# A 32-head attention kernel with a gated MLP: prologue by tile with TensorE transposes, vector work kept off the head boundaries, last out-projection split by head

## Chip, cores, metric

One core of one Trainium2 chip. Times are device microseconds (us) of that core. Most runs of one kernel lie within 0.3% of each other; in two kernels (a_spq and a_best) one run lies up to 0.6% off. Every run quoted here was in the fast state. "Span" is the profiled time from the first to the last instruction, about 2 us less than that run's time. "Pitch" is the time from the start of one matmul to the start of the next.

## The reference, cut to what matters

```python
xn = layernorm(A_x)                                   # 2048 x 512
q = xn @ wq                                           # 32 heads of 128
p = softmax(q @ k_cache^T * 128**-0.5)                # per head, 2048 x 2048
s = concat_heads(p @ v_cache) @ wo                    # 2048 x 512
h = relu(xn @ w1 + b1) ** 2;  g = silu(h @ w2 + b2)   # F = 1792
return A_x + s * g                                    # bf16
```

## The kernel before

The queries come in 4 blocks of 512 rows. In each block all 32 heads are done in turn, each in 8 steps of 256 keys, so there are 1024 steps. A step is a pair of score matmuls (into `psA`), an exponential of 1024 elements per partition on ScalarE (into `pT`), and eight PV matmuls of 129 columns (into `psO`; the extra column of ones gives the softmax denominator). PV runs two steps behind the scores. Between scores and PV, TensorE takes "fillers": matmuls of the projections, the MLP and the output projection, in groups of 4, 8 or 14 into two PSUM banks (`psF`), each group ended by an eviction on VectorE (it reads the finished bank, so that the bank can be filled again). A "combine" is VectorE's last arithmetic on a row tile of the output: times the gate `g`, plus `A_x`.

```python
# the prologue: the whole block of 512 rows in one go
ln_load(0); fill_wq(0); fill_k(0); fill_wq(1)         # all on SP's DMA queue
ln_stats(0)                                           # 4 x bn_stats/bn_aggr, one power on GpSimd
ln_scale(0, range(TPB))                               # 4 x scale, each followed by a DMA transpose
fill_v(0); fill_k(1); fill_v(1); fill_wq(2)
tok_w1 = ...                                          # w1 in one transfer, then w2
# [cut: projections of heads 0 and 1]

for pi in range(NPAIR):                               # the 1024 steps
    g, k = divmod(pi, NPR)
    gen_scores(pi)
    credit = min(credit + left[0] / (NPAIR - pi), 8.0)
    n = 0
    while n < 3:
        late = bool(jobs) and jobs[0][0] + 8 <= pi
        if not (credit >= 1.0 or late) or n == 2 or not fill_one(pi):
            break                                     # fill_one: one filler; evicts after a group's last
        ...
    if pi >= LAG:
        gen_pv(pi - LAG)      # after a head's last PV: VectorE copies psO to o_un, frees psO
    # [cut: loads of later heads]
    for fn in events.pop(pi, []):                     # statistics, scalings, gates, combines
        fn()
# after the loop: the last PVs, the transpose of the last head, then what is left,
# 4 jobs of 8 matmuls (one for each 128 rows), one after the other
while jobs or cur[0] is not None or events:
    for fn in events.pop(step, []):
        fn()
    fill_one(step, force=True)
    step += 1
```

Every instruction goes into its engine's queue in this program order. VectorE's trace shows it working in that order: at the head boundary at 100 us in the kernel before, the copy to `o_un` starts at 99.58 us, behind four statistics and a cast, though the PV matmuls that it waits for ended at 97.5.

The softmax here doesn't subtract the row's maximum and nothing guards it: scores larger than these inputs give would overflow.

Of the kernel before, what the change touches and what calls it, by code (L numbers as in the profile page):

```python
# [9 lines left out]
P = 128  # L10
# [177 lines left out]


def _bn_stats(e, out, in_):  # L190
    return e.bn_stats(out, in_)  # L191
# [19 lines left out]
def bass_recurrent_scan__mha_block_cached__dense_activation_squared_relu__prompt_kernel(  # L211
# [70 lines left out]
    ve_t = sb("ve_t", [P, TPB], F32)  # L282
    mhalf = sb("mhalf", [P, TPB], F32)
    rstd = sb("rstd", [P, TPB], F32)
# [13 lines left out]
    sl_wq = [S.slot(f"wq{i}") for i in range(NSW)]  # L298
    sl_xl = S.slot("xl")
    sl_xT = [S.slot(f"xT{i}") for i in range(TPB)]  # L300
    sl_w1 = S.slot("w1")
    sl_w2 = S.slot("w2")
# [6 lines left out]
    sl_fin = [S.slot("fin0"), S.slot("fin1")]  # L309

    t_mhalf = E(GP, partial(_memset, out=mhalf[:], val=-0.5))
    t_ones = None
    for i in range(NSL):
        t_ones = E(GP, partial(_memset, out=v_sb[:, i, :, Dh:Dh + 1], val=1.0))


    t_xl = [None] * NQB
    t_xn_w = [None] * NQB
    tok_xT = [[None] * TPB for _ in range(NQB)]
    t_xr = [None] * NQB  # L320

    def ln_load(j):
        t_xl[j] = S.emit_dma(
            SP, partial(_dma, out=x_ln[:], in_=A_x[0, j * QB:(j + 1) * QB, :].rearrange(
                "(t p) d -> p t d", p=P)), sl_xl, deps=[t_xn_w[j - 1] if j else None])

    def ln_stats(j):
        t = None
        for i in range(TPB):
            ts_ = E(DV, partial(_bn_stats, out=st_t[:, i, :], in_=x_ln[:, i, :]),  # L330
                    deps=[t_xl[j], t_xn_w[j - 1] if j else None])
            t = E(DV, partial(_bn_aggr, out=mv_t[:, i, :], in_=st_t[:, i, :]), deps=[ts_])
        t = E(DV, partial(_ts, out=ve_t[:], in0=mv_t[:, :, 1], scalar1=LN_EPS, scalar2=None,
                          op0=ALU.add), deps=[t, t_xr[j - 1] if j else None])
        t_xr[j] = E(GP, partial(_tt, out=rstd[:], in0=ve_t[:], in1=mhalf[:], op=ALU.pow),
                    deps=[t, t_mhalf, t_xn_w[j - 1] if j else None])

    def ln_scale(j, tiles):
        for i in tiles:
            t_xn_w[j] = t = E(DV, partial(_ts, out=xn_t[:, i, :], in0=x_ln[:, i, :],  # L340
                                          scalar1=mv_t[:, i, 0:1], scalar2=rstd[:, i:i + 1],
                                          op0=ALU.subtract, op1=ALU.mult),
                              deps=[t_xr[j], tok_xT[j - 1][i] if j else None])
            jt = j * TPB + i
            tok_xT[j][i] = S.emit_dma(
                SP, partial(_dmaT, out=xnT[:, :, jt * P:(jt + 1) * P], in_=xn_t[:, i, :]),
                sl_xT[i], deps=[t])

# [23 lines left out]

    def fill_v(g):
        if g >= NG:
            return
        h, i, prev = g % H, g % NSL, g - NSL
        t_vfill[g] = S.emit_dma(
            SP, partial(_dma, out=v_sb[:, i, :, 0:Dh],
                        in_=A_v_cache[0, h].rearrange("(t p) d -> p t d", p=P)), sl_v[i],
            deps=[t_PV_last[prev] if prev >= 0 else None])  # L380

    def fill_wq(g):
        if g >= NG:
            return
        h, i, prev = g % H, g % NSW, g - NSW
        t_wqfill[g] = S.emit_dma(
            SP, partial(_dma, out=wq_sb[:, i, :, :],
                        in_=A_wq[:, h * Dh:(h + 1) * Dh].rearrange("(c p) e -> p c e", p=P)),
            sl_wq[i], deps=[t_proj[prev] if prev >= 0 else None])
# [88 lines left out]
    dbg = os.environ.get("KDBG")  # L478

    def at(step, fn):  # L480
        events.setdefault(step, []).append(fn)
# [20 lines left out]
    def job_h(j, c):  # L502
        js = slice(j * QB, (j + 1) * QB)
        box = [None]

        def mm(n, bank):
            box[0] = E(PE, partial(_mm, out=bankF(bank), lhsT=w1_sb[:, n, c * P:(c + 1) * P],
                                   rhs=xnT[:, n, js], start=(n == 0), stop=(n == NDC - 1)),
                       deps=[tok_w1, t_bankF[bank]] + tok_xT[j], inc=(n == NDC - 1))

        def evac(bank, step):
            s = c % 2
            t1 = E(DV, partial(_ts, out=r_t[:, s, :], in0=bankF(bank), scalar1=b1f[:, c:c + 1],
                               scalar2=0.0, op0=ALU.add, op1=ALU.max),
                   deps=[box[0], t_b1, t_rt[s]])
            t_h2[j, c] = t_rt[s] = E(
                DV, partial(_tt, out=h2T[:, c, :], in0=r_t[:, s, :], in1=r_t[:, s, :],
                            op=ALU.mult),
                deps=[t1] + [t_o2.get((j - 1, qt)) for qt in range(TPB)])
            return t1  # L520
        return NDC, mm, evac
# [34 lines left out]
    def job_wo(j, m, qt):  # L556
# [4 lines left out]
        def mm(n, bank):  # L561
            g = g0 + n
            box[0] = E(PE, partial(_mm, out=bankF(bank),
                                   lhsT=oT[:, g % NOT, qt * P:(qt + 1) * P],
                                   rhs=wo_all[:, m * HC + n, :], start=(n == 0),
                                   stop=(n == HC - 1)),
                       deps=[tok_wo[m], tok_oT[g], t_bankF[bank]], inc=(n == HC - 1))

        def evac(bank, step):
# [5 lines left out]
            elif m < NCH - 1:  # L575
                t_acc[qt] = t = E(DV, partial(_tt, out=acc[:, qt, :], in0=bankF(bank),
                                              in1=acc[:, qt, :], op=ALU.add),
                                  deps=[box[0], t_acc[qt]])
            else:
                s = jt % 2  # L580
                t = E(DV, partial(_stt, out=tmp_t[:, s, :], in0=bankF(bank), scalar=0.5,
                                  in1=g_all[:, jt % (2 * TPB), :], op0=ALU.mult, op1=ALU.mult),
# [18 lines left out]
    def pre_combine(j, qt):  # L601

        jt = j * TPB + qt
        t = E(DV, partial(_stt, out=acc[:, qt, :], in0=acc[:, qt, :], scalar=0.5,
                          in1=g_all[:, jt % (2 * TPB), :], op0=ALU.mult, op1=ALU.mult),
              deps=[t_acc[qt], t_g[jt]])
        t_u[jt] = E(DV, partial(_tt, out=acc[:, qt, :], in0=acc[:, qt, :], in1=x_t[:, qt, :],
                                op=ALU.add), deps=[t, tok_xt[jt]])
# [4 lines left out]
    for j in range(NQB):  # L613
        b = j * (SPB - NPR)
        for c in range(NFC):
# [6 lines left out]
        for m in range(NCH):  # L622
            for qt in range(TPB):
                r = b + HC * NPR * (m + 1) + 14
                jobs.append((r + 2 + 12 * qt, r, job_wo(j, m, qt)))
    jobs.sort(key=lambda x: x[0])
    cur = [None]
    bank_no = [0]

    def fill_one(step, force=False):  # L630
# [15 lines left out]
        else:  # L646
            cur[0][1] = i + 1
        return True


    ln_load(0)
    fill_wq(0)
    fill_k(0)
    fill_wq(1)
    ln_stats(0)
    ln_scale(0, range(TPB))
    fill_v(0)
    fill_k(1)
    fill_v(1)
    fill_wq(2)  # L660
    tok_w1 = S.emit_dma(SP, partial(_dma, out=w1_sb[:],
                                    in_=B_w1.rearrange("(c p) f -> p c f", p=P)), sl_w1)
    tok_b1 = S.emit_dma(GP, partial(_dma_gather, nc, out=b1b[:],
# [4 lines left out]
    for g in range(2):  # L668
        n, mm, evac = job_proj(g)
        for i in range(n):  # L670
            mm(i, g)
        t_bankF[g] = evac(g, 0)
    t_b1 = E(DV, partial(_copy, out=b1f[:], in_=b1b[:]), deps=[tok_b1])
    tok_w2 = S.emit_dma(SP, partial(_dma, out=w2_sb[:],
                                    in_=B_w2.rearrange("(c p) d -> p c d", p=P)), sl_w2)
    for i in range(NCH):
        at(3 * NPR + 6 + 2 * NPR * i, partial(load_wo, i))
    for j in range(NQB):
        if j + 1 < NQB:
            at(j * SPB + 3 * NPR, partial(ln_load, j + 1))  # L680
            at(j * SPB + 7 * NPR, partial(ln_stats, j + 1))
            for i in range(TPB):
                at(j * SPB + 10 * NPR + 6 + NPR * i, partial(ln_scale, j + 1, [i]))
        at(j * SPB + SPB // 2, partial(load_xt, j))
        for qt in range(TPB):
            at(j * SPB + SPB + 4 + 2 * qt, partial(pre_combine, j, qt))

    left = [sum(job[0] for _, _, job in jobs) - HC * TPB]
    credit = 0.0
    for pi in range(NPAIR):  # L690
# [3 lines left out]
        n = 0  # L694
        while n < 3:
            late = bool(jobs) and jobs[0][0] + 8 <= pi
            if not (credit >= 1.0 or late) or n == 2 or not fill_one(pi):
                break
# [3 lines left out]
        if dbg:  # L702
            print(pi, n, round(credit, 1), jobs[0][0] if jobs else None)
        if pi >= LAG:
# [6 lines left out]
        if k == LAG + 1 and g >= 1:  # L711
            gen_oT(g - 1)
        for fn in events.pop(pi, []):
            fn()
    for pi in range(NPAIR - LAG, NPAIR):
        gen_pv(pi)
    gen_oT(NG - 1)
    step = NPAIR
    while jobs or cur[0] is not None or events:
        for fn in events.pop(step, []):  # L720
            fn()
        fill_one(step, force=True)
        step += 1
    assert not jobs and cur[0] is None and not events

# [32 lines left out]
```

## Time and profile before

| | before |
|---|---|
| time, median of 3 runs | 1290.23 us (1288.71 to 1290.77) |
| span of the profiled run (a run of 1287.63 us) | 1285.8 us |
| first score matmul starts | 20.34 us |
| from there to the start of the last PV matmul | 1247.85 us |
| from there to the end of the last output sum | 12.95 us |
| from there to the end | 4.71 us |

The last four rows add up to the span. They are read from the timeline and are used for every run below: first scores = the prologue, stretch = the 1024 steps, end = the last output projection, rest = the last store.

### The profile page before, as it was taken

The numbers are of one execution on the slowest core, as the hardware profiler recorded it, in microseconds if no ns is written. First come the engines' busy times: TensorE is split into PE (matmuls) and PEld (weight loads), VectorE is DVE, ScalarE is ACT, GpSimd is POOL, SyncE is SP. The second block draws the span as 40 slices with busy tenths as digits, with TensorE's granted clock in tenths as the row PEclk, the third lists the DMA queues.
The fourth block names the chain that finished last, engine by engine and source line by source line (L and its number), as shares of the span: only waits on it lengthen the run. The fifth ranks groups of instructions, "written<-read, shape, count | busy, mean of one in ns | idle before, by whom it ended". The sixth has DMA issues, their size and how long they took to land.

```text
span 1285.8 us, 26303 instructions
## 1 busy us (share of the span) xinstructions
PE 1231.2 (96%) x11506; PEld 807.6 (63%) x11712; DVE 472.0 (37%) x949; ACT 1052.9 (82%) x1041; POOL 21.6 (2%) x42
## 2 busy tenths in 40 slices
PE   3999999999999999999999999999999999999997
PEld 1665666666666666666666666666666666666664
DVE  2443323323534433322353533332345343233234
ACT  1887888888887888888888888888888878888894
POOL 1000000000001000000000100000000000000000
PEclk8999999999999999999999999999999999999999
DMA  8999787878887897776788877777778778677761
GB/s 195 208 199 211 159 136 140 145 128 140 140 161 146 143 159 127 144 137 127 142 139 160 161 147 141 138 144 130 137 143 135 143 151 143 128 140 137 135 115 29
DMA packets 687089, 185.89 MB, mean 145 GB/s; under 512 B 677088, under 2 KB 685536, under 8 KB 686976
## 3 DMA queue, kind: packets, MB, share of 16 engines
q1 hardware_dynamic: 685536, 180.41, 76.7%
q0 software_dynamic: 1440, 3.81, 1.3%
q8 instruction: 92, 1.51, 0.5%
q14 instruction: 21, 0.17, 0.1%
HBM read 96.08 MB, written 2.10 MB: 76 GB/s over the span
## 4 chain that ended last, share of the span: by engine, by line
PE 93%; DVE 3%; issue 1%; DMA 1%; SPq 1%; POOL 0%
PE psO L157 36%; PE psA L152 33%; PE psF L152 24%; DVE r_t L171 1%; SPq L203 1%; DVE st_t L191 1%; DVE o_un L179 0%; DVE h2T L165 0%; DMA wq_sb<-in_A_wq_dram 0%; DMA x_ln<-in_A_x_dram 0%; DMA oT<-o_bf 0%; DVE mv_t L195 0%; DVE qt_sb L179 0%; DVE xn_t L171 0%; DVE acc L175 0%
## 5 line engine op out<-in xcount | busy, mean ns | idle before, releaser
L161 ACT ACTIVATE pT<-psA 128x1024 bf16<-128x1024 f32 x1024 | 1044.9, 1023 | 214.1 <-PE psA L152 170.4
L157 PEld LDWEIGHTS psO<-v_sb,pT 128*128 128x128 bf16 x8192 | 546.4, 98 | 268.8 <-issue 39.4
L157 PE MATMUL psO<-v_sb,pT 128*128 128x129 bf16 x8192 | 638.9, 220 | 13.2 <-DVE o_un L179 11.9
L152 PE MATMUL psA<-qt_sb,kT 128*128 128x512 bf16 x1849 | 567.2, 380 | 10.4
L152 PE MATMUL psF<-xnT,wq_sb 128*128 128x512 bf16 x510 | 177.0, 385 | 22.2 <-DMA xnT<-xn_t 17.1
L179 DVE COPY o_un<-psO 128x258 f32<-128x258 f32 x256 | 97.0, 421 | 229.6 <-PE psO L157 228.5
L152 PE MATMUL psF<-wo_all,oT 128*128 128x512 bf16 x510 | 170.2, 383 | 2.6 <-DMA oT<-o_bf 2.5
L152 PEld LDWEIGHTS psA<-qt_sb,kT 128*128 128x128 bf16 x2048 | 158.6, 98 | 1.3 <-issue 1.3
L179 DVE CAST qt_sb<-psF 128x512 bf16<-128x512 f32 x128 | 88.4, 691 | 190.9 <-PE psF L152 190.8
L152 PEld LDWEIGHTS psF<-xnT,wq_sb 128*128 128x128 bf16 x512 | 50.5, 99 | 84.1 <-issue 19.5
L152 PEld LDWEIGHTS psF<-wo_all,oT 128*128 128x128 bf16 x512 | 50.4, 99 | 64.2 <-DMA oT<-o_bf 3.0
L165 DVE TENSOR_TENSOR o_bf<-o_un,rden 128x512 bf16<-128x512 f32 x128 | 88.6, 692 | 4.6 <-DVE rden L183 0.3
L171 DVE TENSOR_SCALAR r_t<-psF,b1f 128x512 bf16<-128x512 f32 x56 | 42.0, 751 | 125.2 <-PE psF L152 125.2
L152 PE MATMUL psF<-xnT,w_sb 128*128 128x512 bf16 x224 | 76.1, 379 | 0.1
L152 PE MATMUL psF<-w_sb,h2T 128*128 128x512 bf16 x221 | 73.0, 379 | 0.0
L165 DVE TENSOR_TENSOR acc<-psF,acc 128x512 f32<-128x512 f32 x32 | 22.1, 690 | 94.5 <-PE psF L152 94.5
L152 PEld LDWEIGHTS psF<-xnT,w_sb 128*128 128x128 bf16 x224 | 21.9, 98 | 26.8 <-DMA w_sb<-in_B_w_dram 0.5
L152 PEld LDWEIGHTS psF<-w_sb,h2T 128*128 128x128 bf16 x224 | 21.9, 98 | 26.4
L165 DVE TENSOR_TENSOR z_t<-psF,b2bc 128x512 f32<-128x512 f32 x16 | 11.1, 691 | 62.4 <-PE psF L152 62.4
L179 DVE COPY acc<-psF 128x512 f32<-128x512 f32 x16 | 11.1, 691 | 60.5 <-PE psF L152 60.5
L165 DVE TENSOR_TENSOR h2T<-r_t 128x512 bf16<-128x512 bf16 x56 | 23.8, 426 | 1.9
L183 DVE RECIPROCAL rden<-o_un 128x4 f32<-128x4 f32 x128 | 22.9, 179 | 4.4
(23 smaller groups left out, 109.5 us busy)
## 6 DMA issues: line engine op xcount, KB each, us to landing
v_sb<-in_A_v_cache_dram SPq DMA_DIRECT2D x128, 512.0 KB, 4.8
wq_sb<-in_A_wq_dram SPq DMA_DIRECT2D x128, 128.0 KB, 3.1
wo_all<-in_A_wo_dram SPq DMA_DIRECT2D x4, 1024.0 KB, 6.2
w_sb<-in_B_w_dram SPq DMA_DIRECT2D x2, 1792.0 KB, 9.8
x_ln<-in_A_x_dram SPq DMA_DIRECT2D x4, 512.0 KB, 4.6
kT<-in_A_k_cache_dram SPq DMA_TRANSPOSE x128, 4.6
oT<-o_bf SPq DMA_TRANSPOSE x128, 3.9
x_t<-in_A_x_dram POOLq DMA_DIRECT2D x16, 128.0 KB, 3.5
```

What stands on the lines that cost most here:

```text
L152: return e.matmul(out, lhsT, rhs, start=start, stop=stop)
L157: return e.matmul(out, lhsT, rhs, start=start, stop=stop, skip_group_check=True)
L161: return e.activation(out, in_, func, bias=bias, scale=scale)
L165: return e.tensor_tensor(out, in0, in1, op)
L171: return e.tensor_scalar(out, in0, scalar1=scalar1, scalar2=scalar2, op0=op0, op1=op1)
L179: return e.tensor_copy(out, in_)
L183: return e.reciprocal(out, in_)
L191: return e.bn_stats(out, in_)
L203: return e.dma_start(out, in_, transpose=True)
```

## The change

The intent: (1) take the first block in four tiles of 128 rows, transpose them on TensorE (the result is copied from PSUM by ScalarE), and keep TensorE's clock up with dummy matmuls; issue the first wq and V loads from ScalarE's queue and w1 in quarters. (2) Keep VectorE free for the `o_un` copy: no filler group may end in a head's second step (k == 1), where its eviction would be queued ahead of that copy; up to three fillers in the third step; events only from the third step on, two at a time; the statistics of later blocks tile by tile. (3) At the end, the matmuls of the first seven heads for all four row tiles first, in four banks, then those of the last head; the combines of earlier parts go earlier.

```diff
+        view = psA[:, i * 512:i * 512 + 256].bitcast(BF16)          # ln_scale, block 0
+        for c in range(NDC):
+            t = E(PE, partial(_peT, out=view[:, c * P:(c + 1) * P],
+                              in_=xn_t[:, i, c * P:(c + 1) * P], ident=ident[:]), ...)
+        tok_xT[0][i] = E(AC, partial(_act, out=xnT[...], in_=view..., func=ACT.Copy), deps=[t])
# [cut: ln_load, ln_stats, ln_scale take one tile; warm_up(n): n matmuls of zeros]
-    ln_load(0)
-    fill_wq(0)
+    for i in range(TPB):
+        ln_load(0, i)
     fill_k(0)
-    fill_wq(1)
-    ln_stats(0)
-    ln_scale(0, range(TPB))
-    fill_v(0)
+    fill_wq(0, AC)
+    fill_wq(1, AC)
+    fill_v(0, AC)
+    fill_wq(2, AC)
+    fill_v(1, AC)
+    warm_up(10)
+    for i in range(TPB):
+        ln_stats(0, i)
+        if i >= 2:
+            ln_scale(0, i - 2)
+            warm_up(3)
+    for i in range(TPB - 2, TPB):
+        ln_scale(0, i)
+        if i < TPB - 1:
+            warm_up(2)
     fill_k(1)
# [cut: w1 in four transfers; w2 and wo issued later]
-        while n < 3:
+        most = 3 if k == 2 else 2
+        while n < most:
             late = bool(jobs) and jobs[0][0] + 8 <= pi
-            if not (credit >= 1.0 or late) or n == 2 or not fill_one(pi):
+            if not (credit >= 1.0 or late):
+                break
+            if k == 1 and cur[0] is not None and cur[0][1] == cur[0][0][0] - 1:
+                break
+            if not fill_one(pi):
                 break
-        for fn in events.pop(pi, []):
-            fn()
+        pending.extend(events.pop(pi, []))
+        if k >= 2:
+            for fn in [pending.pop(0) for _ in range(min(2, len(pending)))]:
+                fn()
# [cut: the MLP's jobs start 10 steps later; combines follow the third quarter of the out-projection]
+    places = [bankF(bank_no[0]), bankF(bank_no[0] ^ 1), psA[:, 0:512], psA[:, 512:1024]]
+    for i, (_, _, (n, mm, evac)) in enumerate(tail):
+        for x in range(n - 1):
+            mm(x, (places[i], waits[i]))
+    for i, (_, _, (n, mm, evac)) in enumerate(tail):
+        mm(n - 1, (places[i], waits[i]))
+        evac((places[i], waits[i]), step)
```

## The prediction

> **What bounds the kernel now.** I read the page first, then the waits of TensorE, then the timeline of the first 30 us and of the end, and last the timeline around the places where the waits fall. The page's engine line and its row of slices:
>
> ```profile
> PE 1231.2 (96%) x11506; PEld 807.6 (63%) x11712; DVE 472.0 (37%) x949; ACT 1052.9 (82%) x1041; POOL 21.6 (2%) x42
> PE   3999999999999999999999999999999999999997
> ```
>
> TensorE is the bound everywhere but in the first slice and, a little, the last. ScalarE has 18% in hand, VectorE 63%. So the change can gain only what TensorE loses: it removes no matmul of the body. First, how much is lost. The chain of waits in a quiet stretch shows one step (a pair of score matmuls, one filler matmul, eight PV matmuls):
>
> ```profile
> 1246.34 0.43 PE psA L152 x2
> 1246.77 0.22 PE psF L152
> 1246.98 0.45 PE psO L157 x8
> 1247.44 0.43 PE psA L152 x2
> ```
>
> Start to start is 1.10 us. A filler is 0.2155 us (half of the 0.43 of two), so a step is 0.885 us plus 0.2155 for each filler. By the code there are 1024 steps and, inside the loop, 126x4 + 56x4 + 16x14 + 60x8 = 1432 fillers (the last output projection comes after it): 1024 x 0.885 + 1432 x 0.2155 = 906 + 309 = 1215 us. The first score matmul starts at 20.34 us and the last PV ends at about 1268.2, which is 1248 us. So TensorE loses about 33 us inside the loop, 20.3 before it, and 17.6 come after it. The waits of TensorE name the losses but not their whole size, since a matmul's modelled end lies behind the moment at which the next could have started (0.38 us long, 0.2155 apart):
>
> ```profile
> PE psF L152 <- DMA xnT<-xn_t: 17.1, 1, 17.1
> PE psO L157 <- DVE o_un L179: 11.9, 16, 2.5
> PE psF L152 <- DMA wq_sb<-in_A_wq_dram: 5.1, 1, 5.1
> PE psF L152 <- DMA oT<-o_bf: 2.5, 1, 2.5
> ```
>
> Start (timeline): one load of x lands only at 5.0, four statistics follow, one power on GpSimd, four scalings, and four DMA transposes that land at 17.06. The matmuls after it are 0.43 apart, half speed:
>
> ```profile
> 5.01 0.69 DVE L191 BATCH_NORM_STATS2 st_t<-x_ln 128x6 f32<-128x512 bf16 x1 [5.01 <-DMA x_ln<-in_A_x_dram]
> 8.60 1.04 POOL L165 TENSOR_TENSOR rstd<-ve_t,mhalf 128x4 f32<-128x4 f32 x1 [7.52 <-DVE ve_t L170]
> 9.68 1.94 DVE L171 TENSOR_SCALAR xn_t<-x_ln,mv_t,rstd 128x512 bf16<-128x512 bf16 x4 [1.17 <-POOL rstd L165]
> 10.12 5.15 SPq L203 DMA_TRANSPOSE xnT<-xn_t  x4
> 17.06 3.44 PE L152 MATMUL psF<-xnT,wq_sb 128*128 128x512 bf16 x8 [17.06 <-DMA xnT<-xn_t]
> ```
>
> Head boundaries (timeline around 100 us): the first PV of a head (third step of a head) overwrites the accumulator that VectorE must first copy to o_un. VectorE works in the order of the program, and here 3.2 us of statistics and a cast stand ahead of the copy:
>
> ```profile
> 98.69 0.18 DVE L195 BATCH_NORM_AGGREGATE mv_t<-st_t 128x2 f32<-128x6 f32 x1
> 98.98 0.68 DVE L179 CAST qt_sb<-psF 128x512 bf16<-128x512 f32 x1
> 99.58 0.75 DVE L179 COPY o_un<-psO 128x258 f32<-128x258 f32 x2
> 100.14 0.76 PE L157 MATMUL psO<-v_sb,pT 128*128 128x129 bf16 x8 [2.21 <-DVE o_un L179]
> ```
>
> I took the length of every step from the starts of its score matmuls and subtracted 0.885 + 0.2155 x its fillers. Only the third steps of heads are long: 34 of them lose over 0.15 us, 22.1 us together (nine lose 0.20, ten 0.42, thirteen 0.6 to 1.0, two 2.5 and 2.8); the other boundaries lose 0.05 at most. In the large ones, what ran just ahead of the copy is the eviction of a filler group that ended in the second step (cast 0.69, or r_t and h2T 1.18), or the statistics.
>
> End: the last head's transpose lands at 1272.4, 25 matmuls follow, the first ones cold again, then two VectorE operations:
>
> ```profile
> 1269.95 2.43 DMA oT<-o_bf
> 1272.42 7.27 PE psF L152 x25
> 1279.72 0.70 DVE tmp_t L175
> 1280.44 0.69 DVE out_t L165
> ```
>
> **What the Trainium skill says.** (1) "TensorE: Matmul & The Clock Gate", section "What's actually happening": the array runs at half clock after an idle window of some 3.4 us and at full clock after a busy one. The trace agrees: 0.43 us pitch after the 17 us wait, 0.2155 later, and the granted clock from 26 to 31 us, after the wait of 5.1 us, is 0.55 (the table by windows). (2) The same page, "Part 4: PE-mode transpose": a 128x128 transpose against an identity goes to PSUM, so a copy follows, some 275 to 390 ns alone, and it does not count as activity for the clock. Nothing in this trace shows it. (3) "ScalarE: Activation LUTs", "What ACT_TABLE_LOAD costs": an ACTIVATE is 186 ns + 0.833 ns per element. For the exponentials, 1024 wide, that is 1039 ns; the trace has 1023. So the copy of a 512-wide tile should be 0.61 us. (4) "DMA: Bandwidth & Descriptors", "Issuing engines are not separate DMA queues": issuing from ScalarE saves only issue time. The trace shows why this could still help: SP's one issue of a kT transpose holds its queue 3.4 to 4.6 us.
>
> **The change, part by part.**
>
> *Prologue.* Four loads of 128 KB, issued about 0.5 us apart (0.46 each now), should land from about 3.5 us on (3.5 is also the median of the 128 KB x_t loads). VectorE per tile: statistics 0.66, aggregate and epsilon about 0.35, so 1.05; a scaling is 1.94/4 = 0.49. Its order is three statistics, scale, statistics, three scales: 3.5 + 3x1.05 + 0.49 + 1.05 + 3x0.49 = 9.7 us. The power (1.04 us) hides behind the next tile but for perhaps 0.1. Then the last tile: four transposes with latency 0.5, copy 0.65: projections may start at about 11.0. Eight projection matmuls are 1.7 us warm, 3.4 cold, so the first scores fall at 12.7 to 14.5; warming matmuls cover half of the time between 6 and 10 us, and transposes may not count, so I take 13.5. Against 20.34 this gives **6.8 us**. Nothing of the added work is on another path: ten warming matmuls cold are 4.3 us, over before the first transpose at about 7.
>
> *First steps.* Now 7.8 us are lost in the first 20 steps: 5.1 for wq of the third head, queued behind a K transpose and a V load, and some 2.5 of cold clock after it. wq and V now go out by ScalarE's queue at the start, so that wait goes. In its place the first filler of the MLP, in the fourth step (about 17 us), needs the first quarter of w1. Ahead of it are x, two K, two V and three wq, 2.9 MB. At 4.6 us for each K transpose and about 390 GB/s (best slice of the trace, 26 to 31 us) for the rest, it lands at some 17 to 18. I leave 3.5 of the 7.8: gain **4.3 us**.
>
> *Head boundaries.* A filler group may no longer end in a head's second step, events wait until the third step and come two at a time, statistics come tile by tile, and three fillers may run in the third step, which gives VectorE another 0.2 to 0.4 us. Every large loss I looked at has one of these two causes. Left over: an MLP eviction at the end of the first step, or two events at the end of a head (up to 2.8 us of VectorE). I leave 1.6 of 22.1 us, and take another 1 us from the boundaries of 0.05: gain **21.5 us**.
>
> *End.* All 28 matmuls of the first seven heads run before the wait, 28 x 0.2155 = 6.0 us from 1268.2, past the landing at 1272.4 (4.2 us after), so the wait and the cold clock go. But then four last matmuls meet VectorE with 8 operations of 0.72 = 5.8 us: 6.0 + 0.2 + 0.25 + 5.8 = 12.25 us to the last output, against 1281.13 - 1268.2 = 12.9 now. VectorE takes the place of TensorE: gain **0.7 us**.
>
> Sum: 6.8 + 4.3 + 21.5 + 0.7 = 33.3 us. 1290.2 - 33.3 = **1257 us**.
>
> **Rivals.** (a) The DMA engines become the prologue's bound: they are nearly full from 20 to 40 us already, the same bytes now compete with x, and a K or w1 that is late stalls TensorE, which also goes cold. For: 2.9 MB ahead of w1. Against: in the first 20 us of the kernel before they moved only 131 GB/s (the table by windows), so there is room, and its trace has no wait for K. It would cost 3 to 8 us: 1260 to 1265. (b) VectorE's work is only moved: deferred events pile up in the third step, so a filler bank is evicted late and TensorE waits for the bank. For: after o_un, rden and o_bf (1.7 us) up to an eviction and two events (4 us) may follow, about what two filler groups last. Against: VectorE is 37% busy and such coincidences are few. It would give back 3 to 10 us: 1260 to 1267. (c) Everything goes as meant, warm from the start and no w1 wait: 1250 to 1252.
>
> **Range and chances.** The boundary term is the largest and the best founded; the prologue terms may be 5 us off either way. 80% range 1249 to 1267. Faster by over 2% needs under 1264.4, that is, 26 of the 33 us: 0.86. Within 2%: 0.13. Slower: 0.01.
>
> **What would show it.** Right: first scores at 12.5 to 14.5 us; TensorE's wait for o_un near zero; no wait for wq or oT; the last-ended chain closing with VectorE's tmp_t and out_t pairs in a row. Wrong: waits of psF for w_sb over 3 us, or of psF for VectorE evictions; half clock in the first steps; first scores after 16 us.

## The result

The changed kernel takes 1253.8 us (median of 4 runs, 1252.41 to 1255.12), the kernel before 1289.47 in the same session (1287.13 to 1290.77). The ratio is 0.9725, 95% interval 0.9705 to 0.9746. Ratios here are the mean time of one kernel's fast runs over that of the other's of the same rounds, so not quite the ratio of the medians quoted. The outputs agree with the reference, as in every run below.

The page of the changed kernel, engines and the row of slices. The first slice has filled up. The 99% for TensorE is a little flattered: this is the only profile in which no score matmul record is missing (199 are in the kernel before), and the runs below with the same stretch read 97 or 98%. Before, it was 96%.

```profile
PE 1235.7 (99%) x11746; PEld 812.1 (65%) x11746; DVE 473.5 (38%) x961; ACT 1051.3 (84%) x1045; POOL 27.6 (2%) x57
PE   8999999999999999999999999999999999999996
```

TensorE's waits in the changed kernel (what waited, for what; us in total, times, longest). All of them lie in the prologue or the first steps; `o_un`, `wq`, `oT` and `xnT<-xn_t` are gone from the list:

```profile
PE psA L196 <- DVE xn_t L171: 2.8, 2, 1.6
PE psF L152 <- POOL mhalf L187: 1.3, 1, 1.3
PE psF L152 <- ACT xnT L161: 0.8, 1, 0.8
PE psA L152 <- ACT pT L161: 0.3, 1, 0.3
```

The chain that ended last, its pieces at the start (start, length, what):

```profile
2.13 5.93 DMA x_ln<-in_A_x_dram
...
10.17 1.28 PE psF L152 x3
11.45 0.43 PE psA L196 x4
11.88 0.85 PE psF L152 x2
...
13.81 1.89 PE psF L152 x8
```

The fourth tile of x takes 5.9 us to land. Then come transposes (`psA L196`) and, between them, five dummy matmuls (`psF L152 x3`, `x2`) of 0.43 us each, where a matmul of this size takes 0.2155 at full clock: the clock is at half (by the trace from 9.35 to 12.76 us), so the work meant to keep it up stands on the path. It is full again for the eight projection matmuls (1.89 us). And at the end:

```profile
1233.92 3.02 PE psF L152 x14
1236.94 3.02 PE psA L152 x14
1239.96 0.23 PE psF L152
1240.22 0.70 DVE tmp_t L175
...
1244.92 0.69 DVE out_t L165
```

28 matmuls in a row without a wait, then VectorE's eight operations close the kernel.

Where the 35 us came from, by the same four rows:

| | before | after | gain |
|---|---|---|---|
| first scores start | 20.34 | 15.71 | 4.6 |
| stretch of the 1024 steps | 1247.85 | 1217.99 | 29.9 |
| end | 12.95 | 11.91 | 1.0 |
| rest | 4.71 | 5.10 | -0.4 |
| span | 1285.85 | 1250.71 | 35.1 |

Taking each step's length minus 0.880 us and 0.2155 us for each filler (as in the prediction, with a slightly smaller base, which cancels in a difference), the first 20 steps lost 7.8 us before and -0.4 after: 8.2 us of the 29.9. The other steps lost 29.2 before and 7.2 after (some 22; the stretch leaves 21.7 for them); the third steps of heads alone went from 24.7 to 2.5, and no third step loses more than 0.05 us.

### The profile page after: what moved, and what is told of

Its sections match the earlier page's. It is cut to its first block, busy times and chain, and to the rows that moved or that the text cites. A ratio compares the mean times of both kernels' runs of the same rounds, so it can differ in the third digit from the quotient of the medians.

```text
span 1250.7 us, 26634 instructions
## 1 busy us (share of the span) xinstructions
PE 1235.7 (99%) x11746; PEld 812.1 (65%) x11746; DVE 473.5 (38%) x961; ACT 1051.3 (84%) x1045; POOL 27.6 (2%) x57
## 4 chain that ended last, share of the span: by engine, by line
PE 98%; DVE 0%; DMA 0%; ACT 0%; issue 0%; SPq 0%
PE psO L157 37%; PE psA L152 36%; PE psF L152 25%; DMA x_ln<-in_A_x_dram 0%; DVE tmp_t L175 0%; DVE out_t L165 0%; PE psA L196 0%; SPq L208 0%; ACT pT L161 0%; DVE st_t L200 0%; ACT xnT L161 0%; DVE xn_t L171 0%; DVE mv_t L204 0%; DVE ve_t L170 0%
## 5 line engine op out<-in xcount | busy, mean ns | idle before, releaser
L152 PE MATMUL psA<-qt_sb,kT 128*128 128x512 bf16 x2048 | 609.2, 379 | 0.3 <-ACT pT L161 0.3
L152 PE MATMUL psF<-xnT,wq_sb 128*128 128x512 bf16 x512 | 174.6, 379 | 0.8 <-ACT xnT L161 0.8
L152 PE MATMUL psF<-wo_all,oT 128*128 128x512 bf16 x496 | 164.8, 379 | 0.0
L152 PEld LDWEIGHTS psA<-qt_sb,kT 128*128 128x128 bf16 x2048 | 157.9, 98 | 1.6 <-ACT pT L161 0.7
L152 PEld LDWEIGHTS psF<-xnT,wq_sb 128*128 128x128 bf16 x512 | 50.0, 98 | 61.1 <-issue 0.9
L152 PEld LDWEIGHTS psF<-wo_all,oT 128*128 128x128 bf16 x496 | 48.5, 98 | 58.3
L152 PE MATMUL psF<-xnT,w_sb 128*128 128x512 bf16 x224 | 75.9, 379 | 0.0
L152 PE MATMUL psF<-w_sb,h2T 128*128 128x512 bf16 x224 | 73.8, 379 | 0.0
L152 PEld LDWEIGHTS psF<-xnT,w_sb 128*128 128x128 bf16 x224 | 21.9, 98 | 26.4
L152 PEld LDWEIGHTS psF<-w_sb,h2T 128*128 128x128 bf16 x224 | 21.9, 98 | 26.4
L208 POOL DMA_DIRECT2D out_dram<-out_t x12 | 6.5, 541 | 856.9 <-DVE out_t L165 856.9
```

The lines of the kernel that those rows point to most:

```text
L152: return e.matmul(out, lhsT, rhs, start=start, stop=stop)
L208: return e.dma_start(out, in_)
```

## The experiments

Theory E: the boundaries pay because the eviction of a filler group stood ahead of the `o_un` copy; with the prologue and the first steps, that is the whole gain. Rivals: the events' holding back matters rather than the groups' (G); work that is moved comes back as other waits (M); the DMA engines' bytes, not any queue or engine, set the prologue (D). Some runs have rivals of their own; their letters are explained in the expectations. All 12 runs are told here. The rows of each, from its profile:

| run | median us | first scores | stretch | end | waits of PV for o_un |
|---|---|---|---|---|---|
| before | 1289.47 | 20.34 | 1247.85 | 12.95 | 16, 11.9 us |
| after | 1253.8 | 15.71 | 1217.99 | 11.91 | none |
| b_guard | 1270.63 | 20.0 | 1231.6 | 12.74 | 2, 4.1 us |
| a_noguard | 1269.77 | 18.30 | 1233.57 | 11.92 | 12, 6.7 us |
| a_nogate | 1255.27 | 14.36 | 1219.97 | 11.91 | 2, 1.1 us |
| a_spq | 1258.38 | 12.39 | 1226.87 | 11.91 | none |
| a_dmaT | 1259.19 | 21.83 | 1218.41 | 11.91 | none |
| a_nowarm | 1252.78 | 15.85 | 1218.06 | 11.92 | none |
| a_warm10 | 1252.74 | 15.72 | 1218.38 | 11.91 | none |
| a_xfirst | 1254.09 | 16.85 | 1219.19 | 11.91 | none |
| a_tailseq | 1251.95 | 15.03 | 1218.32 | 11.28 | none |
| a_tailpool | 1253.71 | 17.76 | 1218.41 | 10.76 | none |
| a_order | 1252.92 | 12.33 | 1223.11 | 11.92 | none |
| a_best | 1254.39 | 12.32 | 1222.02 | 10.40 | none |

One caution for reading it: five of these profiles have the changed kernel's prologue untouched (after, a_noguard, a_nogate, a_tailseq, a_tailpool), and their first scores fall anywhere from 14.36 to 18.30 us. The granted clock goes with it: in a_nogate it never fell (14.36), in a_tailseq and in the changed kernel it was at half for 3.41 us (15.03, 15.71), in a_tailpool and a_noguard for 10.24 us (17.76, 18.30). The fourth x tile, which lands at 8.06 to 9.06 us, adds to it. The changed kernel's four runs fall in two pairs, 1252.4 and 1252.6 us with a mean granted clock of 0.996 to 0.997, and 1255.0 and 1255.1 with 0.994; such a spell at half clock may be what sets them apart, but only one of them has a trace. So differences of 2 us in the total are not read below; the rows are. The medians were taken in four sessions whose kernels before had medians of 1288.17 to 1289.72.

### b_guard: the rule for filler groups, on the kernel before

```diff
-        while n < 3:
+        most = 3 if k == 2 else 2
+        while n < most:
...
+            if k == 1 and cur[0] is not None and cur[0][1] == cur[0][0][0] - 1:
+                break
```

> The kernel before with one part of the change alone: a filler group may not end in the second step of a head, and the third step may take three fillers. Theory E (the boundary loss comes from the eviction of a filler group that stands ahead of the o_un copy in VectorE's order): of the 22.1 us lost at 34 boundaries all go but the two that the statistics cause (2.5 and 2.8 us), so 16 to 18 us less than before: about 1272 us, VectorE's o_un as TensorE's releaser down from 11.9 us to about 5, start and end unchanged. Rival M (the load is only moved and comes back as waits for filler banks or for events): at most 8 us less, 1281 or more, with new waits of TensorE for psF evictions.

Measured: 1270.63 us, ratio to before 0.986 (0.9846 to 0.9875). The stretch is 16.2 us shorter. TensorE's wait for the copy, in this run:

```profile
PE psO L157 <- DVE o_un L179: 4.1, 2, 2.5
```

Theory E holds in kind and size: these few lines give half of the gain of the whole change (18 of 36 us), and the two waits left are those behind the four statistics. Nothing came back elsewhere in the stretch, so M falls for the boundaries (the one new wait, 1.3 us for `tmp_t`, lies in the end, which is no longer than before). The edit also allows three fillers in the third step; the next run takes out the rule alone. One of the two waits, 2.50 us at 404 us, was followed by 3.41 us of half clock, another 1.4 us lost; the same wait of 2.50 us in the kernel before was not.

### a_noguard: the changed kernel without that rule

```diff
-            if k == 1 and cur[0] is not None and cur[0][1] == cur[0][0][0] - 1:
-                break
```

> The changed kernel without that rule: a group may end in the second step again; the third step still takes up to three fillers and events still wait. Theory E: 11 to 17 us more than the changed kernel, 1265 to 1271, nearly all of it at third steps, as waits of the first PV for o_un. Rival G (it is the holding back of events that counts): at most 4 us more, under 1258.

Measured: 1269.77 us. The stretch is 15.6 us longer than the changed kernel's; the profiled run's first scores also come 2.6 us later (18.30), which is the prologue's own scatter. The waits are back:

```profile
PE psO L157 <- DVE o_un L179: 6.7, 12, 0.8
```

Shown from both sides, the rule is worth some 16 us. The longest wait is now 0.8 us, not 2.5: the long ones were the statistics.

### a_nogate: events at once

```diff
-        if k >= 2:
-            for fn in [pending.pop(0) for _ in range(min(2, len(pending)))]:
-                fn()
+        for fn in [pending.pop(0) for _ in range(len(pending))]:
+            fn()
```

> The changed kernel with the events (scalings, statistics, gates, combines) emitted at once at their step instead of from a head's third step on and two at a time; the statistics stay one tile at a time, the rule for filler groups stays. Theory E: 0 to 3 us more than the changed kernel, 1254 to 1257. Rival G: 8 us more or worse, 1262 or over, with waits for o_un.

Measured: 1255.27 us, the stretch 2.0 us longer, with two waits of 1.1 us together:

```profile
PE psO L157 <- DVE o_un L179: 1.1, 2, 0.5
```

G falls: holding events back is worth about 2 us. With the statistics still by tile, the two waits of 4.1 us of b_guard do not come back in full. No run takes the statistics by tile alone, but the step lengths say where the remaining 6 us or so of the boundaries lie: the two boundaries behind the four statistics lose 5.0 us in b_guard, besides the 1.4 of half clock; in a_nogate, with statistics by tile, the two largest lose 1.7; in the changed kernel none loses more than 0.05.

### a_spq: the first loads on SP in the old order

```diff
+    fill_wq(0)
     fill_k(0)
-    fill_wq(0, AC)
-    fill_wq(1, AC)
-    fill_v(0, AC)
-    fill_wq(2, AC)
-    fill_v(1, AC)
+    fill_wq(1)
+    fill_v(0)
...
     fill_k(1)
+    fill_v(1)
+    fill_wq(2)
```

> The changed kernel with the first wq and V loads issued by SP in the old order (wq, K, wq, V, then K, V and the third wq after the transposes) instead of by ScalarE. Theory Q (the lost first steps of the kernel before came from wq of the third head standing behind K and V in SP's queue): 3 to 6 us more than the changed kernel, with a wait of psF for wq of about 3 to 5 us after the first scores and half clock after it. Rival D (the queue matters little, since all run on the same DMA engines, and the fourth x tile, which lands at 8.1 us, would even come sooner): between 1 us less and 1 us more.

Measured: 1258.38 us (1258.0 to 1264.85). Theory Q is right on the total, rival D on x. The x tiles land sooner (the fourth at 4.6 us instead of 8.1) and the first scores fall 3.3 us earlier; but then wq of the third head, behind K and V, costs TensorE 6.7 us and its clock:

```profile
12.39 0.59 PE L152 MATMUL psA<-qt_sb,kT 128*128 128x512 bf16 x2
19.70 0.61 PE L152 MATMUL psF<-xnT,wq_sb 128*128 128x512 bf16 x1 [6.71 <-DMA wq_sb<-in_A_wq_dram]
20.09 1.06 PE L152 MATMUL psA<-qt_sb,kT 128*128 128x512 bf16 x2
```

The last line's pair takes 1.06 us where a pair takes 0.59 at full clock. So the changed kernel's loads from ScalarE's queue, which also come in another order, shorten the stretch by 8.9 us and pay for it with 3.3 us of the prologue. That queue and order are not the same thing is seen in a_order below.

### a_dmaT: the first block's transposes by DMA again

```diff
-        if j > 0:
+        if True:
             t_xnr[jt] = tok_xT[j][i] = S.emit_dma(
```

> The changed kernel with the first block's four transposes made by DMA again; all else as changed (tile by tile, warming matmuls, loads by ScalarE). Theory P (the PE path is what shortens the prologue, since a DMA transpose queues behind the K transposes and takes 3 us to land): first scores 3 to 7 us later than the 15.7 of the changed kernel, total 1257 to 1261. Rival S (splitting by tile and early loads do it): within 1 us.

Measured: 1259.19 us, first scores at 21.83:

```profile
18.46 3.57 PE L152 MATMUL psF<-xnT,wq_sb 128*128 128x512 bf16 x8 [10.49 <-DMA xnT<-xn_t]
```

Theory P holds: without the TensorE path the prologue is no shorter than before (21.83 us against 20.34), although everything else in it is by tile. The last scaling ends at 10.47 us, as in the changed kernel (10.36); the last of the four DMA transposes is issued at 12.20, behind K's and the others on SP's queue, and lands at 18.33.

### a_nowarm and a_warm10: the dummy matmuls

a_nowarm issues none of the 18; a_warm10 only the first ten.

```diff
-        for _ in range(n):
+        for _ in range(0):
             E(PE, partial(_mm, out=bankF(1), lhsT=warm[:, 0:P], rhs=warm[:], ...
```

> The changed kernel without any warming matmul. In the changed kernel the clock went back to half at 9.35 us in spite of them, and five warming matmuls of 0.43 us then stood on the path between the last transposes. Theory W (they pay): half clock in the projections and the first steps costs 1.5 us in the projections and 2 to 3 us after, less 2.1 us for the five that go: 1 to 3 us slower than the changed kernel. Rival N (they don't pay): equal within 0.7 us, or up to 1.5 us faster; first scores at about 15 us.

> The changed kernel with only the first ten warming matmuls, not those between the transposes. By theory W it is the late ones that bring the full clock at 12.76 us, just before the projections: without them the projections take 3.4 us instead of 1.9 and the first steps run at half clock, though the last transposes come 2 us sooner: 0 to 2 us slower. By rival N 0.5 to 1.5 us faster.

Measured: 1252.78 and 1252.74 us, first scores at 15.85 and 15.72. Rival N holds: in the changed kernel the dummies gain nothing. TensorE's timeline of the run without any:

```profile
10.12 1.46 PE L196 MATMUL psA<-ident,xn_t 128*128 128x128 bf16 x12 [2.56 <-DVE xn_t L171]
12.48 3.57 PE L152 MATMUL psF<-xnT,wq_sb 128*128 128x512 bf16 x8 [0.90 <-ACT xnT L161]
```

The projections run at half clock (3.57 us against 1.89), but they start 1.3 us sooner, at 12.48 instead of 13.81. With the dummies, what they are worth hangs on the clock. In a_nogate, with all 18 of them, it stayed full:

```profile
12.46 1.89 PE L152 MATMUL psF<-xnT,wq_sb 128*128 128x512 bf16 x8 [0.78 <-ACT xnT L161]
```

From the end of the last scaling to the first scores it took 4.94 us without dummies (a_nowarm), 3.80 with dummies and full clock (a_nogate), 5.35 in the changed kernel, whose clock was at half until 12.76 us, and 6.94 in a_noguard and a_tailpool, where it was at half until after 18 us. So the dummies win 1.1 us if the clock holds and lose up to 2.0 if it falls. Of the profiles whose fourth x tile lands after 8 us, with late dummies in place, it held in one of six. In the four where x lands by 5.5 us (a_spq, a_xfirst, a_order, a_best) it held to the first scores every time, so there the dummies may pay; no run took them out there.

### a_xfirst: K and V held back until x has landed

```diff
+    S.emit_wait(SP, [t_xl[3]])
     fill_k(0)
     fill_wq(0, AC)
     fill_wq(1, AC)
+    S.emit_wait(AC, [t_xl[3]])
     fill_v(0, AC)
```

> The changed kernel, with the first K transpose and ScalarE's loads from V on held back until the four x tiles have landed. In the changed kernel the fourth x tile landed at 8.06 us, 5.9 after its issue, and the statistics waited for it 1.2 us of their own and their order. Theory X (x competes with K, V and wq for the DMA engines): x lands by 5.5 us, the fourth scaling is done by about 9.5, first scores 1 to 2.5 us sooner than 15.7. Rival K: K of the first head then lands after 14 us and takes x's place as the bound, so first scores come no sooner, or later.

Measured: 1254.09 us. x did land at 5.4 us and the last scaling ended at 8.88, but the projections started only at 12.51: ScalarE, which had its own loads to issue until 9.0 us and then a table load, made its first copy only at 10.30. Then rival K:

```profile
16.85 0.60 PE L152 MATMUL psA<-qt_sb,kT 128*128 128x512 bf16 x2 [2.46 <-DMA kT<-in_A_k_cache_dram]
```

K of the first head landed at 16.8 us, 11.4 us after its issue, with V, wq and the next head's K beside it; in the kernel before it landed 5.6 us after its issue, with x and wq beside it. The 14 profiles fall into two groups: 4.9 to 5.8 us in the five where V was issued at least 3 us after K (before, b_guard, a_spq, a_order, a_best), 9.3 to 12.0 in the nine where V went out before K or with it. So what is under way next to it counts most.

### a_tailseq: the end in the old form

```diff
-    for i, (_, _, (n, mm, evac)) in enumerate(tail):
-        for x in range(n - 1):
-            mm(x, (places[i], waits[i]))
...
+    jobs = tail
+    while jobs or cur[0] is not None:
+        fill_one(step, force=True)
+        step += 1
```

> The changed kernel with its last output projection in the old form, one block of rows after the other, eight heads each, in the two filler banks; the combines stay early. In the changed kernel 11.9 us lie between the start of the last PV and the last output. Theory T (the split by head fills the wait for the last transpose): TensorE waits again some 2.5 us for oT, comes back at half clock, and 25 matmuls stand after the wait, but VectorE has no combines left to do, so 0.5 to 1.5 us more. Rival V (VectorE's chain of eight operations sets the end either way): within 0.3 us.

Measured: 1251.95 us; the end takes 11.28 us, against 11.91 with the split. Neither theory: the old form is shorter by 0.6 us. Its chain:

```profile
1237.61 5.58 PE psF L152 x25
1243.22 0.70 DVE tmp_t L175
1243.94 0.69 DVE out_t L165
```

TensorE does wait for the last transpose, but afterwards it finishes one row tile every 1.7 us and VectorE follows it, so only two operations stand at the end. The split ends all four tiles together and leaves eight. The half clock that I expected did not come in this profile; in the kernel before it did (25 matmuls in 7.27 us there, 5.58 here). With the split TensorE does not wait before these matmuls, and its clock stayed full there; with the old form it fell in one of three profiles (the kernel before, not b_guard or this run). This run's other times are 1251.58, 1252.32 and 1255.54 us, the last with a mean granted clock of 0.993 against 0.997 to 0.999; where its clock fell isn't known. What the old form with the combines still in it costs at full clock is seen in b_guard, whose clock did not fall either: 12.74 us, with VectorE's combines in the chain between the tiles:

```profile
1257.61 0.69 DVE acc L175
1258.93 0.70 DVE acc L175
```

So the combines that left the end are worth some 1.5 us, and the split costs 0.6 of it back.

### a_tailpool: another order at the end, two sums on GpSimd

```diff
# [cut: front(i) is the seven heads of row tile i, finish(i) its last head and eviction]
+    for i in range(3):
+        front(i)              # seven heads of tiles 0, 1, 2
+    finish(0); finish(1)      # the last head, eviction
+    front(3)
+    finish(2); finish(3)
...
+                ea = GP if jt in (NQB * TPB - 4, NQB * TPB - 2) else DV
```

> The changed kernel with another order at the end: seven heads of three blocks, then the last head of two of them, which VectorE starts on 1.3 us earlier, then the rest; and the final sums of blocks 0 and 2 on GpSimd. Theory V' (VectorE's eight operations of 0.67 us are the end's bound): the last output comes 1.3 us sooner by the order and up to 1.4 more by GpSimd, so 10.5 to 9.2 us after the start of the last PV instead of 11.9. Rival: the last transpose lands later than the 21 matmuls end, or GpSimd is slow (over 1.5 us for one sum), then nothing is gained.

Measured: end 10.76 us, 1.15 less than the split, where 1.3 to 2.7 were expected. The order gains; GpSimd does not (the same order without it, in a_best, takes 10.40). First one of its two sums, then VectorE's own sum beside it, from the timeline:

```profile
1241.95 1.26 POOL L165 TENSOR_TENSOR out_t<-tmp_t,acc 128x512 bf16<-128x512 f32 x1 [231.73 <-DVE tmp_t L175]
```

```profile
1242.50 1.27 DVE L165 TENSOR_TENSOR out_t<-tmp_t,acc 128x512 bf16<-128x512 f32 x1
```

GpSimd needs 1.26 us for a sum of 0.69 on VectorE, and VectorE's own two sums beside GpSimd's take 1.27 and 1.30. The Trainium skill ("SBUF — State Buffer", section "SBUF: two separate sides") says that a VectorE operation with two SBUF inputs and a GpSimd one that reads SBUF exclude each other for the whole instruction. The trace agrees in the main: VectorE's sum of 1242.50, which starts second, ends at 1243.77, 0.56 us after GpSimd's ends at 1243.21. A sum alone takes 0.69, so a small part of it ran or was made ready beside GpSimd's. Besides, both last sums waited for a store to free one of only two `out_t` slots.

### a_order: first loads on SP in the order of need

```diff
# [shortened]
-    fill_k(0) ... fill_v(1, AC); fill_k(1)
+    fill_wq(0); fill_k(0); fill_wq(1); fill_wq(2); fill_v(0)
...
     # w1 in quarters; after the first one:
+        if i == 0:
+            fill_k(1); fill_wq(3); fill_v(1)
# [cut: in the loop, wq of the fourth head is not issued again]
```

> The changed kernel with all first loads on SP in the order of need: x, wq, K of the first head, two wq, V of the first head, the first quarter of w1, then K, wq, V of later heads, then the rest of w1. In the run with SP in the old order the first scores fell at 12.4 us, 3.3 sooner, and 6.7 us were lost to wq of the third head; in the run that held K back, K of the first head became the bound at 16.8. Theory O (it is the order in which the bytes are asked for, not which engine asks): first scores at 12 to 13 us, no wait over 1 us after them, 2.5 to 3.5 us less than the changed kernel: 1250 to 1251.5. Rival: V of the first head or w1 is late by 2 us or more, and nothing is gained.

Measured: 1252.92 us. The first scores did fall at 12.33, and V of the first head came in time, but the gain went again, as the stretch is 5.1 us longer: 0.9 us for w1 in the fourth step, and at 51 us a wait of 2.0 us, followed by 3.41 us of half clock:

```profile
53.33 0.69 PE L152 MATMUL psF<-xnT,wq_sb 128*128 128x512 bf16 x2 [2.04 <-DMA wq_sb<-in_A_wq_dram]
```

This wq stood behind w2, one transfer of 1.8 MB issued at 40.6 us that landed at 52.0. In the changed kernel a wq lands just behind w2 as well, at 49.6 us, but TensorE begins on the next projection only at 53.5.

### a_best: that order, w2 in four pieces, the better end

```diff
# [shortened]
-    at(2 * NPR, load_w2)                  # one transfer
+    for i in range(4):
+        at(28 + 16 * i, load_w2)          # a quarter each
# with a_order's loads, and a_tailpool's end without GpSimd
```

> The changed kernel with the first loads in the order of need on SP (as in the run before, whose first scores fell at 12.3 us but which lost 2.0 us and a spell of half clock at 51 us to a wq load that stood behind the one transfer of all of w2), w2 in four pieces spread over 48 steps, and the end in the better order (the last head of two blocks right after seven heads of three; no GpSimd). Theory O (the order of the bytes asked for sets the start, and the loss at 51 us was w2's one transfer): first scores at 12 to 13 us, no wait for wq, stretch from the 20th step as in the changed kernel (1195 us), last output 10.6 us after the start of the last PV instead of 11.9: 3.5 to 4.7 us less than the changed kernel, about 1249 to 1250 us, ratio to before about 0.969. Rival D (the DMA engines are full for the first 80 us, so what is gained at the start comes back as a wait elsewhere): the wait only moves, 1252 to 1254 us.

Measured: 1254.39 us over five runs, from 1249.93 to 1257.43; ratio 0.9736 (0.9713 to 0.9759). It is not faster than the changed kernel. The profile is of the run of 1251.68 us. The end is 10.40 us (10.6 was expected), and the first scores 12.32. The wait at 51 us is gone, and others stand in its place, for w1 at 17 us and for wq at 128 us:

```profile
PE psF L152 <- DMA wq_sb<-in_A_wq_dram: 1.9, 2, 1.7
PE psF L152 <- DMA w_sb<-in_B_w_dram: 1.3, 1, 1.3
```

This fits rival D. The wq at 128 us was issued behind 1 MB of wo (landed at 125.5) and a DMA transpose (126.1), another such meeting. Why the five runs lie up to 7.5 us apart, one profile doesn't tell; the two with the lower mean granted clock (0.996 against 0.998) are the slowest, so spells of half clock may be a part of it. No version of mine beats the changed kernel beyond the noise; a_tailseq (ratio 0.9723) and a_nowarm (0.9721) match it with less code.

## Why the prediction was right

The predicted time was 1257.0 us, the measured 1253.8, within the range. The largest term was right in cause and size. That the sum came so close is partly luck: the prologue was 2.2 us too large and the first steps 3.9 us too small. By its terms:

| term | predicted gain | measured |
|---|---|---|
| prologue | 6.8 | 4.6 |
| first steps | 4.3 | 8.2 |
| head boundaries | 21.5 | about 22 |
| end | 0.7 | 1.0, and -0.4 in the rest |
| sum | 33.3 | 35.1 (spans) |

**Head boundaries: right in cause and size.** b_guard and a_noguard show the eviction ahead of the copy as cause of 16 us, the statistics as that of the two longest waits. What I left over (an eviction at the end of the first step, two events at the end of a head) did not show: no third step loses more than 0.05 us. The other 6 us or so of the 22 lie at the two boundaries behind the statistics; that taking these by tile wins most of it is read from step lengths (5.0 us in b_guard, 1.7 in a_nogate) and not from a run of its own. Rival (b), banks evicted late, did not happen: there is no wait of psF for VectorE in the list.

**Prologue: right in mechanism, too large.** First scores fell at 15.71 us, not at 13.5, which is neither in the window that I had set for right (12.5 to 14.5) nor past the mark for wrong (16). Two steps fail. The first is the term "3.5 + 3x1.05 + ...", which took the four x tiles to land one after the other from 3.5 us on. The first three did (3.39, 4.35, 5.29), the fourth landed at 8.06, since K, wq and V were under way beside it; a_spq, with V behind, has it at 4.6. The last scaling thus ended at 10.36 us instead of 9.7, although the power on GpSimd took only 0.55 to 0.65 us for one column instead of the 1.04 that I took over from four. The reading behind it, that 131 GB/s in the first 20 us leaves room, was wrong: the same row of that table has the DMA engines busy for 0.71 of those 20 us. The second is "Nothing of the added work is on another path: ten warming matmuls". The change has 18, and eight of them stand between the transposes in TensorE's order. The clock fell at 9.35 us, five of them then cost 2.1 us on the path, and from the last scaling to the projections it took 3.45 us where I had 1.3. "Warming matmuls cover half of the time" was a doubt in the right place; the projections themselves took 1.9 us, less than the 2.5 that I allowed for it. That TensorE's transposes are what shortens the prologue is shown by a_dmaT.

**First steps: right in cause, undersized.** The step that fails is "I leave 3.5 of the 7.8" us, for a w1 that would come too late. The first quarter of w1 did land where I put it (17.8 us), but the first scores came 2.2 us later than I had said, so it was needed only at 19.2. The two errors offset each other in part, and by no merit of the prediction: a later start costs nothing where the next transfer would have been waited for. a_order shows the other side, with first scores at 12.3 and a wait for w1. And wq of the third head, which a_spq shows to be the old loss, was never waited for.

**End: the size nearly right, the cause partly wrong.** I said that VectorE takes TensorE's place as the bound, and it does. But I booked the gain on the matmuls ahead of the wait; a_tailseq and b_guard show that it is the combines that left the end, and that the split itself, at full clock, loses 0.6 us.

**Rival (a)**, the DMA engines, was not the total's bound, but the prologue now runs against them, as far as four runs tell: a_spq, a_xfirst, a_order and a_best each moved a wait from one transfer to another, and none lowered the sum beyond the noise. Rival (c), everything as meant, came half true: no wait for w1, but not warm from the start.

## What to carry to other kernels

Where an in-order engine frees a buffer that the bottleneck needs, look at what stands ahead of that one instruction in its queue, not at the engine's share of busy time: VectorE was 37% busy and cost 22 us, and one condition won 16 of them back. At a start where every transfer is wanted at once, changing the order moves the wait, so add up the bytes ahead of each need before expecting a gain. Measure parts of a change one by one even if the whole is right: of this one, the dummy matmuls bought nothing, with x landing as late as it did, and the split of the end lost 0.6 us.

## What the Trainium skill lacked or had wrong

- "TensorE: Matmul & The Clock Gate", Part 4: it gives a transpose of 128x128 bf16 as some 275 to 390 ns. Here a record is mostly 314 ns long at half clock (a_nowarm) and 219 at full (a_nogate), and back to back they start 0.107 us apart at half clock and 0.056 at full. The page gives no such rate for transposes. So they do run at full clock when it is granted; whether they count as activity for the clock gate, no run here decides.
- The same page, Part 1: it doesn't say what dummy matmuls in a kernel's prologue are worth. Here 18 of them gained nothing in the total (1253.8 us with, 1252.78 without); on the prologue they won 1.1 us where the clock held and lost up to 2.0 where it fell in spite of them.
- "DMA: Bandwidth & Descriptors", "Latency and other measured facts": it gives 261 GB/s for a DMA transpose with a non-contiguous middle dimension, and more for a contiguous one. A K transpose of 512 KB here lands 4.6 us after its issue in the median, latency and neighbours included, which is 114 GB/s, so that the page's figure is no estimate of when it lands. And no figure is given for what other transfers under way cost: the first one landed 5.6 us after its issue in the kernel before and 10.4 in the changed one, where V is under way too.
